# Output projection, FFN and q projection of a decode kernel with the weights as the moving operand, in four column tiles

## The chip, the cores and the metric

The kernel runs on one core of a Trainium2 chip. The metric is device time in microseconds (us) for one execution. Engines are named PE (matmul), DVE (vector), ACT (scalar), POOL (general) and SP (here it only issues transfers). A profile's span is some 2 us shorter than the time of the same run. A median is over all runs of a kernel, the slow ones too. A ratio is the mean time of one kernel's fast runs over that of the other's of the same rounds on the same chip, so it is not quite the ratio of the medians that are quoted beside it.

## The reference, cut to what matters

```python
# B = 4 tokens (batch), one position each, D = 448; 16 query heads, 8 KV heads, head size 256
# KV cache: 8192 positions, only the last W = 2048 are used; FFN width 1792; bf16
def A(x):                                # attention on the cache
    q = x @ wq                           # 448 -> 4096
    p = softmax(q @ k_window.T * 256**-0.5)
    return (p @ v_window) @ wo           # 4096 -> 448
def F(x):
    return (silu(x @ w_gate) * (x @ w_up)) @ w_down    # 448 -> 1792 -> 448
x = x + A(layernorm(x)); x = x + F(layernorm(x))
x = x + A(layernorm(x)); x = x + F(layernorm(x))       # same weights, same cache again
```

Two layers use the same cache window. A "pair" below is one token with one KV head in one layer: 1 MB of K and 1 MB of V, 64 pairs in all.

## The kernel before

The kernel is a graph of operations. A small planner, run when the program is built, gives each engine a fixed order. It is a greedy list scheduler: whenever an engine is free in the planner's own clock, it takes the ready operation with the lowest `rank`. The durations are constants in the source.

One pair. K is turned on DVE, the scores of 2048 positions are 32 matmuls, and the softmax goes from engine to engine: maximum on DVE, a broadcast matmul on PE, a second maximum on DVE, two exponentials on ACT. Two PSUM banks `Sb` are shared by all pairs in turn (NS = 2).

```python
MM = 0.0272                                          # planned us of one small matmul
...
g.op(PE, 32 * MM, pos - SLEAD, scores, ...)          # SLEAD = 1.5: before the previous pair's rank
g.op(DVE, 0.12, pos, lambda e: e.tensor_reduce(pmax[s_][:, :], Sb[s_][:, 0:32], AX.X, ALU.max, apply_transpose=True), ...)
g.op(PE, 0.1, pos, lambda e: e.matmul(Sb[s_][:, 128:256], lhsT=pmax[s_][:, 0:1].broadcast_to([128, 128]),
                                      rhs=identb[:, :], start=True, stop=True, ...), ...)        # the broadcast
g.op(DVE, 0.2, pos, lambda e: e.tensor_reduce(negm[s_][:, :], Sb[s_][:, 128:256]..., ALU.max, negate=True), ...)
for n in range(2):
    g.op(SCA, 0.17, pos, lambda e, n=n: e.activation(praw..., Sb..., ACT.Exp, bias=negm[s_][:, n:n + 1]), ...)
...
def pv(e, hv):                                       # already in four column tiles: V moves past 4 columns of p
    for a in range(2):
        for gg in range(4):
            last = e.matmul(Yb[p_][32 * gg:32 * gg + 4, 256:512], lhsT=pT..., rhs=half[vs[hv][0]]..., ...)
```

The small projections have the weights stationary, a 128x128 load for each matmul of 1 to 4 columns (the profile counts 5728 loads for 5728 matmuls in the whole kernel):

```python
def out_proj(pos, si, pairs):
    def emit(e):
        for cc in range(4):
            c0 = 128 * cc if cc < 3 else D - 128
            for k in range(4):
                last = e.matmul(Av[:, cc, sl], lhsT=wo_sb[:, 4 * kvh + k, c0:c0 + 128],
                                rhs=oT[si % 2][:, k % 2, k // 2, 0:n], start=False, stop=False, ...)
        return last
    g.op(PE, 16 * MM, pos, emit, ...)
...
def residual(t, rank):
    vec(rank, lambda e: e.tensor_tensor(xs[:, t, :], xs[:, t, :], Av[:, :, t], op=ALU.add), ...)
...
# when a token has finished a layer's 8 heads (rank CROSS = 20 positions ahead):
residual(t, pos); norm(t, pos, True)
if layer == 0:
    ffn(with_ + [t], pos)                            # gate, up 2 x 56 matmuls, down 56
    norm(t, pos, False)
    qproj([t], ((h0, 1), (h0 + 1, 1), (h0 + 2, HKV - h0 - 2), (0, h0)), pos)   # 128 matmuls, first head first
```

Transfers go into 15 buffers ("halves") of 512 KB. Five heads of each token stay in SBUF for the second layer; a held V half comes free when the second layer's pair has read it. The second layer of a token begins three steps into the next token.

Of the kernel before, what the change touches and what calls it, by code (L numbers as in the profile page):

```python
# [5 lines left out]
ACT = mybir.ActivationFunctionType  # L6
# [38 lines left out]
DSTART = 2.1  # L45
TAIL = {"pe": 0.2, "dve": 0.12, "act": 0.15, "pool": 0.1, "sp": 0.05}
# [232 lines left out]
def build(nc, A_x, A_k_cache, A_v_cache, A_wq, A_wo, B_x, B_w_gate, B_w_up, B_w_down, out):  # L279
# [3 lines left out]
    with ExitStack() as es:  # L283
# [12 lines left out]
        onesb = sb("onesb", [128, 128], BF16)  # L296
        rab = sb("rab", [128, 129], BF16)
        ra = [rab[:, 1:129], rab[:, 0:128]]
        esel = sb("esel", [128, 4, 4, 32], BF16)
        small = sb("small", [128, 9 + 2 * NS + 4 * NY], FP32)  # L300
# [5 lines left out]
        qmask = sb("qmask", [128, 4], BF16)  # L306
        qc = [sb(f"qc{t}", [128, HKV, 8, 2], BF16) for t in range(B)]
        qe = [sb(f"qe{i}", [128, 8, 4, 2], BF16) for i in range(NQ)]
        qS = sb("qS", [128, 8, 16], BF16)
        xio = KT[NKT - 1][:, 0:D]  # L310
        xio_k = tuple(f"kt{NKT - 1}_{hf}_{q}" for hf in range(2) for q in range(TRP))
        xs = sb("xs", [128, B, 4], FP32)
        st = sb("st", [128, B, 16], FP32)
# [4 lines left out]
        th = sb("th", [128, 2 * NFC], FP32)  # L318
        t1 = sb("t1", [128, 2 * NFC], FP32)
        hT = sb("hT", [128, 2 * NFC], BF16)  # L320
        pmax = [sb(f"pmax{s}", [128, 1], BF16) for s in range(NS)]
# [3 lines left out]
        osel = sb("osel", [128, 2], BF16)  # L325
        oT = [sb(f"oT{s}", [128, 2, 2, 2], BF16) for s in range(2)]
# [8 lines left out]
        Av = Ab[:, 0:16].rearrange("p (c t) -> p c t", t=B)  # L335

        R0 = -100.0
        MM = 0.0272
# [13 lines left out]
        def c_fill(e):  # L352
            e.memset(onesf[:, :], 1.0)
            e.memset(expo[:, 0:1], -0.5)
            e.memset(expo[:, 1:3], -1.0)
            e.memset(wrow[:, 0:3], 1.0 / D)
            e.memset(wrow[0:64, 3:4], 0.0)
            e.memset(wrow[64:128, 3:4], 1.0 / D)
            e.memset(qmask[:, :], 0.0)
            return e.memset(Ab[:, 0:16], 0.0)  # L360

        g.op(DVE, 0.5, R0, c_fill, w=("onesf", "expo", "wrow", "qmask") + tuple(f"acc{t}" for t in range(B)), bank=("A",))
# [6 lines left out]
        for a in range(4):  # L369
            g.op(DVE, 0.2, R0, lambda e, a=a: e.tensor_copy(  # L370
                esel[:, :, a, :], identb[:, :].rearrange("p (c s) -> p c s", c=4)), r=("identb",), w=(f"esel{a}",))
# [6 lines left out]
        for p_ in range(NY):  # L378
            g.op(DVE, 0.27, R0, lambda e, p_=p_: e.memset(Yb[p_][:, 256:512], 0.0), w=(f"y{p_}",), bank=(f"Y{p_}",))
        g.op(DVE, 0.2, R0, lambda e: e.memset(rab[:, :], 0.0), w=("ra",))  # L380
        g.op(DVE, 0.2, R0, lambda e: e.tensor_copy(
            rab[:, 1:129].rearrange("p (u v) -> p v u", v=2)[:, 0, :], identb[:, 64:128]), r=("identb",), w=("ra",))

# [10 lines left out]
        load(-80, 1 << 19, wq_sb[:, 3 * 4096:], A_wq[384:448, :].rearrange("r (h n) -> (r h) n", h=2), "wq3")  # L394
# [6 lines left out]
        def load_ffn(rank, rank_d):  # L401
            for nm, wsb, src in (("wg", wg_sb, B_w_gate), ("wu", wu_sb, B_w_up)):
                load(rank, 3 * 458752, wsb[:, 0:3 * FF].rearrange("p (c n) -> p c n", c=3),
                     src[0:384, :].rearrange("(c p) n -> p c n", p=128), nm + "a", 3584)
                load(rank, 229376, wsb[:, 3 * FF:], src[384:448, :].rearrange("r (h n) -> (r h) n", h=2), nm + "b")
            load(rank_d, 1605632, wd_sb[:, :, :], B_w_down.rearrange("(c p) n -> p c n", p=128), "wd", 896)
# [5 lines left out]
        def norm(t, rank, for_ffn):  # L412
# [3 lines left out]
            vec(rank, lambda e: e.scalar_tensor_tensor(out=s[:, 4:8], in0=xs[:, t, :], scalar=1.0, in1=wrow[:, :],  # L416
                                                       op0=ALU.mult, op1=ALU.mult, accum_out=s[:, 0:1]),
                (f"x{t}", "wrow"), (k + "w",), 0.18)
            vec(rank, lambda e: e.scalar_tensor_tensor(out=s[:, 4:8], in0=s[:, 4:8], scalar=1.0, in1=xs[:, t, :],
# [6 lines left out]
            vec(rank, lambda e: e.tensor_scalar(xn[:, :, t], xs[:, t, :], Z2[:, 0:1], None, op0=ALU.subtract),  # L426
# [3 lines left out]
            def spread(e):  # L430
                e.matmul(Z2[:, 16:17], lhsT=ra[0], rhs=xn[:, 3, t:t + 1], start=True, stop=False,
                         skip_group_check=True)
                return e.matmul(Z2[:, 17:18], lhsT=ra[1], rhs=xn[:, 3, t:t + 1], start=False, stop=True,
                                skip_group_check=True)
            g.op(PE, 0.06, rank, spread, r=(f"xn{t}", "ra"), w=("z2",), bank=("Z2",))
            vec(rank, lambda e: e.tensor_copy(xe[:, :, t], Z2[:, 16:18]), ("z2",), (f"xe{t}",), 0.1, ("Z2",))

# [7 lines left out]
            if for_ffn:  # L445
                gp(lambda e: e.tensor_single_scalar(s[:, 11:12], s[:, 8:9], 0.5, op=ALU.mult), (k + "r2",), (k + "s",))
                gp(lambda e: e.tensor_scalar(s[:, 14:15], s[:, 8:9], s[:, 11:12], None, op0=ALU.mult),
                   (k + "r2", k + "s"), (k + "t",))
# [5 lines left out]
        def qproj(ts, chunks, rank):  # L454

            n, sl = len(ts), span(ts)
            rn, rx = tuple(f"xn{t}" for t in ts), tuple(f"xe{t}" for t in ts)
            for i, (h0, nh) in enumerate(chunks):
                zb, z, bank = (Zb, "z", "Z") if i % 2 == 0 else (Z2, "z2", "Z2")

                def q_mm(e, zb, h0, nh, c0, c1):
                    last = None
                    for cc in range(c0, c1):
                        for hh in range(2 * nh):
                            for ee in range(2):
                                o = zb[:, (hh * 2 + ee) * n:(hh * 2 + ee + 1) * n]
                                if cc < 3:
                                    base, rhs = cc * 4096 + (2 * h0 + hh) * 256, xn[:, cc, sl]
                                else:
                                    h_ = 2 * h0 + hh  # L470
                                    base, rhs = 3 * 4096 + (h_ % 8) * 256, xe[:, h_ // 8, sl]
                                lhsT = wq_sb[:, base:base + 256].rearrange("p (m v) -> p v m", v=2)[:, ee, :]
                                last = e.matmul(o, lhsT=lhsT, rhs=rhs, start=(cc == 0 and hh == 0 and ee == 0),  # L473
                                                stop=(cc == 3), skip_group_check=True)
                    return last
                for c0, c1, rr, kw in ((0, 3, rn, dict(w=(z,))), (3, 4, rx, dict(acc=(z,)))):
                    g.op(PE, 4 * nh * (c1 - c0) * MM, rank,
                         lambda e, zb=zb, h0=h0, nh=nh, c0=c0, c1=c1: q_mm(e, zb, h0, nh, c0, c1),
                         r=rr + tuple(f"wq{c}" for c in range(c0, c1)), bank=(bank,), **kw)
                for j, t in enumerate(ts):  # L480
                    g.op(SCA, 0.18, rank, lambda e, zb=zb, j=j, t=t, i=i, nh=nh: e.activation(
                        qS[:, i * n + j, 0:4 * nh], zb[:, 0:4 * nh * n].rearrange("p (k t) -> p t k", t=n)[:, j, :],
                        ACT.Copy, scale=st[:, t, 8:9]), r=(z, f"st{t}r2"), w=(f"qS{i}_{j}",), bank=(bank,))
                for j, t in enumerate(ts):
                    def select(e, zb=zb, i=i, j=j, nh=nh):
                        last = None
                        src = qS[:, i * n + j, 0:4 * nh].rearrange("p (k h v) -> p k v h", h=2, v=2)
                        for c in range(4):
                            lhsT = esel[:, c, :, :].rearrange("p a s -> p (a s)")
                            o = zb[:, 128:128 + 16 * nh].rearrange("p (k c x) -> p k c x", c=4, x=4)[:, :, c, :]  # L490
                            last = e.matmul(o, lhsT=lhsT, rhs=src, start=(c == 0), stop=(c == 3),
                                            skip_group_check=True)
                        return last
                    g.op(PE, 0.12, rank, select, r=(f"qS{i}_{j}", "esel0", "esel1", "esel2", "esel3"), w=(z,),
                         bank=(bank,))
                    g.op(DVE, 0.06 + 0.016 * nh, rank, lambda e, zb=zb, h0=h0, nh=nh, t=t: e.tensor_copy(
                        qc[t][:, h0:h0 + nh, :, :].rearrange("p k c h -> p (k c h)"), zb[:, 128:128 + 16 * nh]),
                        r=(z,), w=tuple(f"qc{t}_{h}" for h in range(h0, h0 + nh)), bank=(bank,))

        def ffn(ts, rank):  # L500
            n, sl = len(ts), span(ts)
            gw = NFC * n

# [14 lines left out]
            for gi, (z, bank, w) in enumerate((("z", "Z", "wg"), ("z2", "Z2", "wu"))):  # L518
                g.op(PE, 42 * MM, rank, lambda e, gi=gi: gu(e, gi, 0, 3), r=rn + (w + "a",), w=(z,), bank=(bank,))
                g.op(PE, 14 * MM, rank, lambda e, gi=gi: gu(e, gi, 3, 4), r=rx + (w + "b",), acc=(z,), bank=(bank,))  # L520
# [3 lines left out]
            for j, t in enumerate(ts):  # L524
                g.op(SCA, 0.18, rank, lambda e, j=j, t=t: e.activation(
                    tok(th[:, 0:gw], j), tok(Zb[:, 0:gw], j), ACT.Tanh, scale=st[:, t, 11:12]),
                    r=("z", f"st{t}s"), w=(f"th{j}",), bank=("Z",))
# [295 lines left out]
```

## Time and profile before

| | before |
|---|---|
| time, median of 3 (lowest, highest) | 325.02 us (324.86, 327.12) |
| span of the profile | 322.9 us |
| matmuls, PE busy | 5728, 232.6 us |
| DVE busy, ACT busy | 192.6, 72.4 us |
| moved | 105.27 MB, mean 326 GB/s |

The page of the kernel before: the span, the busy time of the engines, PE and DMA in 40 slices of about 8 us, the rate of the transfers in the same slices, and the queue that the page calls "instruction" (packets, MB, share).

```profile
span 322.9 us, 12873 instructions
...
PE 232.6 (72%) x5728; PEld 169.7 (53%) x5728; DVE 192.6 (60%) x608; ACT 72.4 (22%) x289; POOL 84.9 (26%) x199
...
PE   3654454446588788578796895679787959889875
...
DMA  7999999999999999999889999999899999748000
GB/s 277 399 407 392 393 396 397 391 396 397 391 362 308 338 368 346 400 362 309 301 272 373 375 351 405 355 365 339 277 359 377 357 386 391 277 140 305 5 0 5
...
q8 instruction: 45, 0.74, 0.9%
```

Where transfers run freely they reach 393 to 407 GB/s. At that rate 105 MB need about 265 us (an estimate: 105.27 MB over 397 GB/s). The rest is a start, a tail with no transfers, and dips. The table of 8 us windows of the kernel before shows the dips after the FFN and q of tokens 0 and 1. Its columns are the window, its length, then busy us (instructions) of each engine, the recorded PE clock, the DMA share and GB/s:

```profile
...
core 0: us, PE busy (x) PEld busy (x) DVE busy (x) ACT busy (x) POOL busy (x), PEclk, DMA share, GB/s
...
96.00:104.00 8.00, 6.15 (x178) 4.94 (x178) 4.63 (x14) 1.61 (x7) 1.93 (x5) 1.00 0.88 296
144.00:152.00 8.00, 6.96 (x203) 5.68 (x200) 4.25 (x14) 1.10 (x4) 0.99 (x3) 1.00 0.89 309
152.00:160.00 8.00, 7.56 (x218) 5.95 (x219) 4.51 (x13) 2.34 (x9) 2.33 (x6) 1.00 0.89 313
160.00:168.00 8.00, 6.32 (x153) 4.18 (x149) 2.66 (x14) 2.11 (x9) 2.20 (x5) 1.00 0.81 277
```

The chain of waits of the kernel before has ten pieces over 0.6 us called "issue", 11.2 us in sum. They are of two kinds. In five of them (96.32, 160.25, 215.36, 226.38 and 278.44 us, 6.9 us in sum) PE really stands still for 0.83 to 1.68 us, and these are all such stops of PE over 0.6 us in the trace. The chain of waits of the kernel before has ten pieces over 0.6 us called "issue", 11.2 us in sum. The columns are start, us, what:

```profile
...
95.55 0.77 PE S L637 x29
96.32 1.22 issue
97.54 0.22 PE S L637 x3
```

Here PE stops within one run of 32 score matmuls, 0.2 us after a packet of 16 KB had come on the instruction queue (95.09 to 96.11 us). Such packets come about every 250 PE instructions (45 for 11456 matmuls and loads). That PE waits for instructions there is inferred from these times.

In the other five pieces (106.13, 117.40, 140.86, 194.13 and 248.15 us, 4.3 us in sum) no engine stops: DVE is at work on a transpose of K (L617) all the while, as a piece of the chain and the line of DVE's timeline for the same time show:

```profile
...
194.13 1.13 issue
...
```

```profile
...
194.09 1.25 DVE L617 STREAM_TRANSPOSE KT<-half 128x1024 uint32<-128x1024 uint32 x1 [0.80 <-DMA half<-in_A_k_cache_dram]
...
```

The groups of instructions that the argument needs, from the same kernel (busy us, mean ns of one | idle us before it and what ended it). The broadcast is L649; note 128*4 for the four column tiles of PV, 128*128 for the rest:

```profile
...
L677 PE MATMUL Y<-half,pT 128*4 128x256 bf16 x1024 | 70.0, 403 | 9.6 <-DMA half<-in_A_v_cache_dram 8.7 <-issue 0.8
L637 PE MATMUL S<-qe,KT 128*128 128x8 bf16 x2048 | 64.6, 168 | 22.4 <-DVE KT L617 18.5 <-issue 3.0 <-ACT praw L656 0.7
...
L649 PE MATMUL S<-identb,pmax 128*128 128x128 bf16 x64 | 16.6, 284 | 4.5 <-DVE pmax L646 3.6 <-DVE oT L702 0.7
...
L724 PE MATMUL A<-oT,wo_sb 128*128 128x1 bf16 x352 | 12.6, 166 | 2.3 <-DVE oT L702 2.3
```

The mean of one matmul (168 ns for L637) is longer than the distance to the next one's start, as one starts before the last has ended. What a stream costs is the distance between starts, which I take from the trace: 27 ns for the column matmuls of L637, L724, q and FFN, and about 170 or 213 ns from one group of four PV matmuls to the next.

### The profile page before, as it was taken

To read this page: it belongs to the slowest core of one execution; us is meant where nothing else is said; L and a number is where in the kernel's file an instruction comes from. 1 tells how busy PE (TensorE), PEld (TensorE's weight loads), DVE (VectorE), ACT (ScalarE), POOL (GpSimd) and SP (SyncE) were. 2 spreads that over 40 slices of the span, in tenths; PEclk is the share of its full clock that TensorE was granted. 3 is DMA by queue.
4 is the path that set the end of the run, shared out by engine and by line. 5 is a ranking of instruction groups with operands and counts; after the bars stand their busy time and mean duration, and the time that the engine had idled before them with its cause. 6 is when DMAs were issued, how large, how long until landed. Compare 5 with 4: busy or idle time off the path is not lost.

```text
span 322.9 us, 12873 instructions
## 1 busy us (share of the span) xinstructions
PE 232.6 (72%) x5728; PEld 169.7 (53%) x5728; DVE 192.6 (60%) x608; ACT 72.4 (22%) x289; POOL 84.9 (26%) x199
## 2 busy tenths in 40 slices
PE   3654454446588788578796895679787959889875
PEld 2542322234476465366664653567555636686554
DVE  5386555652145778765447787855377874656332
ACT  1112111111022333211231322113223322123310
POOL 3312111112023223240233331313233413134221
DMA  7999999999999999999889999999899999748000
GB/s 277 399 407 392 393 396 397 391 396 397 391 362 308 338 368 346 400 362 309 301 272 373 375 351 405 355 365 339 277 359 377 357 386 391 277 140 305 5 0 5
DMA packets 42327, 105.27 MB, mean 326 GB/s; under 512 B 3096, under 2 KB 7200, under 8 KB 41888
## 3 DMA queue, kind: packets, MB, share of 16 engines
q1 hardware_dynamic: 42272, 104.45, 88.0%
q8 instruction: 45, 0.74, 0.9%
q14 instruction: 10, 0.08, 0.1%
HBM read 104.44 MB, written 0.00 MB: 323 GB/s over the span
## 4 chain that ended last, share of the span: by engine, by line
DMA 38%; PE 34%; DVE 12%; SPq 7%; issue 5%; ACT 2%; POOL 0%; DVEq 0%
DMA half<-in_A_k_cache_dram 20%; DMA half<-in_A_v_cache_dram 12%; PE Y L677 11%; PE S L637 8%; DVE KT L617 6%; DMA wd_sb<-in_B_w_down_dram 5%; PE Z L473 4%; SPq L389 4%; PE A L724 3%; PE Z L514 3%; DVE oh L691 2%; PE Z L542 2%; SPq L609 2%; DVE small L652 2%; SPq L626 1%
## 5 line engine op out<-in xcount | busy, mean ns | idle before, releaser
L617 DVE STREAM_TRANSPOSE KT<-half 128x1024 uint32<-128x1024 uint32 x88 | 108.3, 1233 | 13.3 <-DMA half<-in_A_k_cache_dram 12.9
L637 PE MATMUL S<-qe,KT 128*128 128x8 bf16 x2048 | 64.6, 168 | 22.4 <-DVE KT L617 18.5
L677 PE MATMUL Y<-half,pT 128*4 128x256 bf16 x1024 | 70.0, 403 | 9.6 <-DMA half<-in_A_v_cache_dram 8.7
L637 PEld LDWEIGHTS S<-qe,KT 128*128 128x128 bf16 x2048 | 59.7, 104 | 30.7 <-DVE KT L617 20.8
L687 POOL TENSOR_TENSOR small<-small 128x2 f32<-128x2 f32 x64 | 44.3, 696 | 113.5 <-DVE small L669 103.3
L656 ACT ACTIVATE praw<-S,small 128x16 bf16<-128x16 f32 x128 | 28.7, 279 | 84.6 <-DVE small L652 83.9
L691 DVE SCALAR_TENSOR_TENSOR oh<-oh,small,Y 128x256 bf16<-128x256 bf16 x64 | 30.1, 472 | 23.9 <-ACT oh L689 23.4
L689 ACT ACTIVATE oh<-Y 128x256 bf16<-128x256 f32 x64 | 24.6, 384 | 74.2 <-PE Y L677 74.2
L641 POOL TENSOR_TENSOR qe<-qc,qmask 128x64 bf16<-128x64 bf16 x64 | 18.6, 294 | 71.3 <-PE S L637 52.3
L677 PEld LDWEIGHTS Y<-half,pT 128*4 128x4 bf16 x1024 | 20.0, 94 | 21.8 <-DMA half<-in_A_v_cache_dram 11.5
L646 DVE TRANSPOSE_TENSOR_REDUCE pmax<-S 128x1 bf16<-128x32 f32 x64 | 13.4, 211 | 27.1 <-PE S L637 25.3
L724 PE MATMUL A<-oT,wo_sb 128*128 128x1 bf16 (+1 forms) x688 | 24.8, 166 | 6.4 <-DVE oT L702 6.1
L724 PEld LDWEIGHTS A<-oT,wo_sb 128*128 128x128 bf16 x688 | 22.2, 105 | 10.5 <-DVE oT L702 8.5
L697 PE MATMUL Y<-osel,oh 128*128 128x2 bf16 x128 | 13.3, 173 | 17.4 <-DVE oh L691 17.2
L652 DVE TENSOR_REDUCE small<-S 128x2 f32<-128x128 f32 x64 | 17.4, 282 | 10.4 <-PE S L649 8.3
L666 ACT ACTIVATE pT<-Y 128x64 bf16<-128x64 f32 x64 | 14.1, 222 | 40.7 <-PE Y L663 40.4
L697 PEld LDWEIGHTS Y<-osel,oh 128*128 128x128 bf16 x128 | 8.8, 111 | 27.0 <-DVE oh L691 24.5
L649 PE MATMUL S<-identb,pmax 128*128 128x128 bf16 x64 | 16.6, 284 | 4.5 <-DVE pmax L646 3.6
L473 PE MATMUL Z<-xn,wq_sb 128*128 128x1 bf16 (+1 forms) x480 | 15.6, 165 | 2.6 <-DMA wq_sb<-in_A_wq_dram 1.9
L473 PEld LDWEIGHTS Z<-xn,wq_sb 128*128 128x128 bf16 x480 | 14.3, 104 | 3.4 <-DMA wq_sb<-in_A_wq_dram 2.0
L669 DVE TENSOR_REDUCE small<-Y 128x2 f32<-128x32 f32 x64 | 11.0, 177 | 7.1 <-ACT pT L666 6.8
L440 POOL TENSOR_SCALAR st<-st 128x1 f32<-128x1 f32 x16 | 4.3, 267 | 41.2 <-DVE st L428 40.7
(76 smaller groups left out, 212.0 us busy)
## 6 DMA issues: line engine op xcount, KB each, us to landing
half<-in_A_k_cache_dram SPq DMA_DIRECT2D x88, 512.0 KB, 7.0
half<-in_A_v_cache_dram SPq DMA_DIRECT2D x88, 512.0 KB, 6.7
wo_sb<-in_A_wo_dram SPq DMA_DIRECT2D x8, 448.0 KB, 12.3
wq_sb<-in_A_wq_dram SPq DMA_DIRECT2D x3, 1024.0 KB, 6.9
wd_sb<-in_B_w_down_dram SPq DMA_DIRECT2D x1, 1568.0 KB, 16.3
wg_sb<-in_B_w_gate_dram SPq DMA_DIRECT2D x1, 1344.0 KB, 14.2
wu_sb<-in_B_w_up_dram SPq DMA_DIRECT2D x1, 1344.0 KB, 14.7
wq_sb<-in_A_wq_dram SPq DMA_DIRECT2D x1, 512.0 KB, 10.4
```

The source lines that it names most:

```text
L473: last = e.matmul(o, lhsT=lhsT, rhs=rhs, start=(cc == 0 and hh == 0 and ee == 0), stop=(cc == 3), skip_group_check=True)
L617: return e.transpose(dst[:, 2 * hf + q * n:2 * hf + q * n + n], src[:, q * n:q * n + n])
L637: last = e.matmul(Sb[s_][:, 8 * gg:8 * gg + 8], lhsT=kt[:, gg, ce // 2, ce % 2, :], rhs=qe[q_][:, ce, :, :], start=(gg == 0 and ce == 0), ...
L641: g.op(POOL, 0.25, pos - SLEAD - 1, lambda e: e.tensor_tensor(qe[q_][:, :, :, :], qc[t][:, kvh, :, :].unsqueeze(2).broadcast_to([128, 8, 4 ...
L652: g.op(DVE, 0.2, pos, lambda e: e.tensor_reduce(negm[s_][:, :], Sb[s_][:, 128:256].rearrange("p (k n) -> p n k", n=2), AX.X, ALU.max, nega ...
L656: g.op(SCA, 0.17, pos, lambda e, n=n: e.activation(praw[s_][:, :].rearrange("p (k n) -> p n k", n=2)[:, n, :], Sb[s_][:, 0:32].rearrange(" ...
L677: last = e.matmul(Yb[p_][32 * gg:32 * gg + 4, 256:512], lhsT=pT[p_][:, 4 * gg + 2 * hv + a, :, :].rearrange("p y n -> p (y n)"), rhs=half[ ...
L687: g.op(POOL, 0.25, pos, lambda e: e.tensor_tensor(ri[p_][:, :], rs[p_][:, :], expo[:, 1:3], op=ALU.pow), r=(f"rs{p_}", "expo"), w=(f"ri{p_ ...
L689: g.op(SCA, 0.28, pos, lambda e: e.activation(oh[p_][:, :], Yb[p_][:, 256:512], ACT.Copy), r=(f"y{p_}",), w=(f"oh{p_}",), bank=(f"Y{p_}",))
L691: g.op(DVE, 0.4, pos, lambda e: e.scalar_tensor_tensor(out=oh[p_][:, :], in0=oh[p_][:, :], scalar=lomask[:, 0:1], in1=Yb[p_][:, 256:512], ...
L697: last = e.matmul(Yb[p_][:, 2 * dh:2 * dh + 2], lhsT=oh[p_][:, :].rearrange("p (m e) -> p e m", e=2)[:, dh, :], rhs=osel[:, :], start=Fals ...
L724: last = e.matmul(Av[:, cc, sl], lhsT=wo_sb[:, 4 * kvh + k, c0:c0 + 128], rhs=oT[si % 2][:, k % 2, k // 2, 0:n], start=False, stop=False, ...
```

## The change

The intent is fewer and longer matmuls. With four tokens at most, an activation has 4 columns. If it is the stationary operand, the weights move past it 448 or 512 columns at a time, and four of these matmuls write to the four 32-row strips of one PSUM bank. Output projection falls from 16 matmuls to 4, gate and up from 112 to 34, q from 128 to 32. Results then lie as rows, in four strips that have to be summed and turned back into columns by further matmuls. The residual sum of the output projection and of the down projection stays in PSUM as rows. The last step of each token's layer, token 3's FFN and the last FFN stay in columns. The planner's cost of a small matmul goes from 0.0272 to 0.04 us.

```diff
+ROWF = (0, 1, 2)
+MMV = 0.04
...
-        MM = 0.0272
+        MM = MMV
...
         def out_proj(...):
+            def row(e):
+                for k in range(4):
+                    last = e.matmul(Ab[32 * k:32 * k + B, 0:D], lhsT=oT[si % 2][:, k % 2, k // 2, :],
+                                    rhs=wo_sb[:, 4 * kvh + k, :], start=False, stop=False, skip_group_check=True)
+            if column:
+                g.op(PE, 16 * MM, pos, col, ...)
+            else:
+                g.op(PE, 0.4, pos, row, ...)
...
+        def rows(t, rank):                      # strips -> columns, as a bf16 high and low part
+            g.op(SCA, 0.55, rank, lambda e: e.activation(wideb[:, 0:D], Ab[:, 0:D], ACT.Copy), ...)
+            vec(rank, lambda e: e.tensor_tensor(wideb[:, 512:512 + D], Ab[:, 0:D], wideb[:, 0:D], op=ALU.subtract), ...)
+            def turn(e):
+                for i in range(2):
+                    for cc in range(4):
+                        c0 = 512 * i + (128 * cc if cc < 3 else D - 128)
+                        last = e.matmul(Zb[:, cc:cc + 1], lhsT=wideb[:, c0:c0 + 128], rhs=rsel[:, t:t + 1], ...)
+            g.op(PE, 0.25, rank, turn, ...)
+            vec(rank, lambda e: e.tensor_tensor(xr[:, t, :], xs[:, t, :], Zb[:, 0:4], op=ALU.add), ...)
...
-        def qproj(ts, chunks, rank):
+        def qproj(ts, rank):                    # two banks of 4 strips x 512, copied by ACT, turned, selected
+                        for j in range(4):
+                            last = e.matmul(zb[32 * j:32 * j + B, 0:512], lhsT=xn[:, cc, :], rhs=wq_sb[:, c:c + 512], ...)
...
+        def ffn_row(ts, rank):                  # gate, up; tanh and two DVE passes over 512; turn; down into the rows
+            g.op(SCA, 0.65, rank, lambda e: e.activation(wide[:, :], Zb[:, :], ACT.Tanh, scale=rvec[:, 2:3]), ...)
+            vec(... wide = (wide + 1) * Zb ...);  vec(... wideb = wide * rvec * Z2 ...)
+            g.op(PE, 0.12, rank, turn, ...);      vec(... hT = Zb[:, 0:64] ...)
+            g.op(PE, 1.5, rank, down, ...)
...
             for t, layer in full:
+                rows(t, pos - CROSS)
+            out_proj(pos, si, pairs, bool(full))
...
-                    ffn(with_ + [t], pos)
+                    if t in ROWF:
+                        ffn_row(with_ + [t], pos)
+                        for u in with_ + [t]:
+                            rows(u, pos)
+                            residual(u, pos)
+                    else:
+                        ffn(with_ + [t], pos)
                     norm(...)
-                    qproj([t], ((h0, 1), (h0 + 1, 1), (h0 + 2, HKV - h0 - 2), (0, h0)), pos)
+                    qproj([t], pos)
```

Cut: the layout of the last 64 rows of the weights, constants, small buffers merged to make room, and a clearing of the oT buffers on POOL.

## The prediction

> **What bounds the kernel now.** Mostly the transfers. The page moves 105.27 MB; 8 us stretches full of transfers run at 393 to 407 GB/s, so the data alone needs about 265 of the 322.9 us. By the table of 8 us windows the other 58 are: about 3 at the start, 25 after 296 us (DMA share 0.27, then 0.01), and 30 in dips after each token's FFN and q projection (88-128, 144-176, 208-240, 248-264, 272-296 us; share 0.61 to 0.95). In the dips PE shows 6.4 to 7.5 us busy of 8, and the DMA queue's own waits are for PE and DVE work that frees K/V halves. Only there and in the tail can this change pay.
>
> **PE cost now (raw start times, groups by line).** A 128x128 load with a 1- or 2-column matmul issues every 27 to 29 ns: output projection 16 in 0.43 us, q 128 in 3.6, FFN 168 in 4.7. Such bursts also use up instructions: an instruction-queue packet of 16 KB comes every ~250 PE instructions (45 packets), and PE shows "issue" gaps of 0.7 to 1.7 us just after such packets in dense bursts (96.3, 106, 117, 141, 160, 194, 215, 226, 278 us), 10.5 us in sum. [...]
>
> **Cost of the new form.** The PV product already uses four column tiles: its groups of four 256-column matmuls start 213 ns apart[...]. [...] Scaled, a group of four takes 0.37 us at 448 columns, 0.43 at 512. Output projection 0.37 against 0.43 (35 of 43 steps: -2 us); q 3.4 against 3.6; FFN about 5 against 4.7. Streaming saves nearly nothing. What falls is matmuls, 5728 to about 4580, instruction packets, 45 to about 36, and the bursts: I expect two thirds of the 10.5 us of gaps to go.
>
> **Added.** Twelve turns of rows (ACT 448 columns ~0.57 us, DVE ~0.65, eight small matmuls, an add: ~2 us of latency; ~8 us of DVE in all); in the three row FFNs a tanh and two DVE passes over 512 columns (~0.7 each) and a turn; in q two copies of ~0.6 and a turn. Residual to first score takes some 5 us longer; three steps (16 us of transfers) lie between, so for tokens 1 and 2 it is partly hidden; token 0's tail behind the down weights (landed 85.4 us) grows 2 us. The last FFN stays in columns; the tail moves under 1.5 us.
>
> **Sum.** -2 (output projection) and -7 (gaps) of PE time, half to three quarters of which reaches the span, +2 for DVE and longer chains, tail -0.5. Some -6 us, with a wide margin since the whole static order changes (the planner's matmul cost goes from 0.0272 to 0.04): **319 us, 311 to 328**; faster 0.45, same 0.46, slower 0.09.
>
> **Right if** matmuls ~4580, instruction packets ~36; PE "issue" gaps over 0.6 us fall from nine to about three; groups of four 512-column matmuls start ~430 ns apart; DMA rate in 144-168 and 208-240 rises by 20 to 40 GB/s; DVE busy +8 us; tail unchanged.
>
> **Wrong if** [...] the gaps aren't fetches; the rows' chain delays second-layer scores so that held halves free later (slower); the new order moves the transfers.

The sizes of the row matmuls are scaled from the measured 213 ns. The durations given for ACT and DVE on 448 and 512 columns were estimates. The trace after has a mean of 541 ns (ACT) and 613 ns (DVE) for 448 columns, 688 ns for the tanh, 662 and 719 ns for the two DVE passes and 687 ns for a copy of q, all of 512. The twelve turns, from ACT's start to the end of the add, take 2.20 to 10.77 us.

## More of the kernel before

On the chip each engine is given its list, with a wait wherever data may be missing. PE keeps to it: in the trace of this kernel the 531 runs of matmuls of one source line start in the order of the program. A wrong duration therefore adds no instruction; it moves instructions in the lists.

```python
# the planner's core (cut)
while n < len(self.ops):
    ...                                              # engine e that can start first, at time t
    o = min((o for o in avail[e] if ready_at[o] <= t + 1e-9), key=lambda o: (o.rank, o.i))
    o.start = t
    free[e] = t + o.dur                              # o.dur: a constant from the source
    o.end = t + o.dur
    ...
    order[e].append(o)                               # the engine's list on the chip
```

## The result, and the profile after

| | before | after |
|---|---|---|
| time, median of 5 (lowest, highest) | 325.02 us (324.15, 327.12) | 351.48 us (348.07, 352.28) |
| ratio, 95% interval | | 1.0789 (1.073 to 1.0847) |
| span of the profile | 322.9 us | 346.0 us |
| matmuls | 5728 | 4584 |
| PE, DVE, ACT busy | 232.6, 192.6, 72.4 us | 238.7, 206.2, 80.3 us |
| "issue" over 0.6 us in the chain of waits | 10, 11.2 us | 5, 5.0 us |
| of these with PE standing still | 5, 6.9 us | none |

The change makes the kernel 8% slower. The same lines of the page as before, and the recorded clock of PE in tenths:

```profile
span 346.0 us, 10675 instructions
...
PE 238.7 (69%) x4584; PEld 138.1 (40%) x4584; DVE 206.2 (60%) x637; ACT 80.3 (23%) x286; POOL 88.1 (25%) x227
...
PE   2654544555497887676877776787796959769855
...
PEclk9999999999995555558665555555655555565555
DMA  7999999999978999899959899999489999626000
GB/s 287 352 401 395 395 393 392 397 367 329 393 283 275 376 367 329 323 346 335 334 202 334 302 396 357 339 360 351 175 289 387 364 327 351 233 69 240 2 1 4
...
q8 instruction: 36, 0.59, 0.7%
```

The counts are as intended, 4584 matmuls and 36 instruction packets, but the transfers have deeper holes. Selected 8 us windows of the changed kernel:

```profile
...
core 0: us, PE busy (x) PEld busy (x) DVE busy (x) ACT busy (x) POOL busy (x), PEclk, DMA share, GB/s
96.00:104.00 8.00, 7.42 (x142) 3.66 (x140) 1.90 (x9) 2.57 (x6) 2.01 (x9) 1.00 0.78 274
...
176.00:184.00 8.00, 6.78 (x162) 4.89 (x159) 7.15 (x23) 2.02 (x8) 3.58 (x11) 0.50 0.52 177
...
248.00:256.00 8.00, 6.72 (x144) 4.47 (x141) 7.13 (x18) 2.03 (x8) 3.22 (x9) 0.50 0.50 168
304.00:312.00 8.00, 5.68 (x159) 4.59 (x159) 7.08 (x22) 1.11 (x5) 4.01 (x13) 0.60 0.32 101
```

The DMA queue's own waits say what it waits for: without the wait of the last store, in sum 149.8 us for DVE and 69.8 for PE, against 121.6 and 79.1 before. DVE must turn K before a K half comes free. In the 8 us ahead of the hole at 176 us it is busy for only 2.7 us, and waits 3.5 us for the matmuls that turn q's rows; in the hole itself it is busy for 7.15 of 8 us.

The time is lost all along. I cut both traces at the addition that ends the first layer of each token (its start on DVE):

| from - to | before | after | difference |
|---|---|---|---|
| start - token 0 | 76.2 us | 77.1 us | 0.9 |
| token 0 - token 1 | 60.2 | 66.9 | 6.7 |
| token 1 - token 2 | 67.3 | 71.9 | 4.6 |
| token 2 - token 3 | 66.3 | 71.1 | 4.8 |
| token 3 - end | 52.9 | 59.0 | 6.1 |

Groups of the changed kernel. 128*4 now stands on the output projection (L838) and q (L488) too; L756 is the broadcast, L644 and L646 make the two parts of the rows:

```profile
...
L838 PE MATMUL A<-wo_sb,oT 128*4 128x448 bf16 x140 | 18.3, 524 | 4.5 <-DVE oT L809 3.4 <-DVE xr L662 1.1
...
L756 PE MATMUL S<-identb,tiny 128*128 128x128 bf16 x64 | 16.0, 288 | 4.7 <-DVE tiny L753 4.6
L488 PE MATMUL Z<-wq_sb,xn 128*4 128x512 bf16 x120 | 14.6, 620 | 0.8 <-DMA wq_sb<-in_A_wq_dram 0.5 <-DVE st L440 0.3
...
L646 DVE TENSOR_TENSOR wide<-A,wide 128x448 bf16<-128x448 f32 x12 | 7.4, 613 | 5.4 <-ACT wide L644 5.4
...
L644 ACT ACTIVATE wide<-A 128x448 bf16<-128x448 f32 x12 | 6.5, 541 | 15.0 <-PE A L578 10.1 <-PE A L838 3.1 <-DVE xr L662 1.8
```

### The clock line, and why it is not the cause

The page says that PE had its full clock before, and half of it from the 13th slice on after. That reading is wrong, and it invites a false story. The trace of the kernel before holds no clock record at all, which is shown as 1.00. The distances give the clock away: a group of four PV matmuls, 256 columns each, starts about 170 or 213 ns after the last, and the longer distance is 1.2 columns a ns. In the changed kernel the first record is at 100.87 us. The record says "full" for six stretches of 3.4 us, each of which begins during a dense burst of rows or within 1.4 us of its end, and the eight distances between PV groups that lie in them are 108 to 110 ns, 2.3 to 2.4 columns a ns; everywhere else they are 166 to 171 or 212 to 215 ns, two or three strays aside, with the record at 0.5 or with no record yet. So by the distances both kernels run PE at half the clock nearly all the time. The run b_burst, below, tests it with a dense burst at the start of the kernel before, since in the changed kernel the record begins with a stretch at the end of one.

This also corrects a reading from the prediction: it took 213 ns as four tiles at only twice the rate of one. They run at once: the four of a group start within 16 ns of each other, and 256 columns in 213 ns is 1.2 columns a ns for each of them, the same as for matmuls that run singly (107 ns from start to start for 128 columns in b_burst). The sizes drawn from it held all the same, since the other groups run at the same 1.2 columns a ns: groups of four 512-column matmuls most often start 427 ns apart.

### The profile page after: what moved, and what is told of

Its sections match the earlier page's. It is cut to its first block, busy times and chain, and to the rows that moved or that the text cites. A ratio compares the mean times of both kernels' runs of the same rounds, so it can differ in the third digit from the quotient of the medians.

```text
span 346.0 us, 10675 instructions
## 1 busy us (share of the span) xinstructions
PE 238.7 (69%) x4584; PEld 138.1 (40%) x4584; DVE 206.2 (60%) x637; ACT 80.3 (23%) x286; POOL 88.1 (25%) x227
## 4 chain that ended last, share of the span: by engine, by line
DMA 40%; PE 34%; DVE 16%; ACT 4%; issue 4%; SPq 3%; POOL 0%; DVEq 0%
DMA half<-in_A_k_cache_dram 21%; DMA half<-in_A_v_cache_dram 19%; PE Y L784 10%; PE S L744 8%; DVE KT L724 7%; PE Z L488 4%; DVE oh L798 2%; PE Z L604 2%; DVE small L759 2%; PE A L838 1%; SPq L716 1%; ACT oh L796 1%; PE Y L804 1%; PE Z L434 1%; PE Y L767 1%
## 5 line engine op out<-in xcount | busy, mean ns | idle before, releaser
L724 DVE STREAM_TRANSPOSE KT<-half 128x1024 uint32<-128x1024 uint32 x88 | 108.2, 1230 | 17.8 <-DMA half<-in_A_k_cache_dram 17.6
L763 ACT ACTIVATE praw<-S,small 128x16 bf16<-128x16 f32 x128 | 27.6, 278 | 60.8 <-DVE small L759 60.2
L753 DVE TRANSPOSE_TENSOR_REDUCE tiny<-S 128x1 bf16<-128x32 f32 x64 | 13.7, 214 | 30.3 <-PE S L744 29.9
L748 POOL TENSOR_TENSOR qe<-qc,tiny 128x64 bf16<-128x64 bf16 x64 | 18.4, 292 | 47.0 <-PE S L744 23.9
L804 PE MATMUL Y<-tiny,oh 128*128 128x2 bf16 x128 | 13.4, 174 | 21.5 <-DVE oh L798 21.3
L838 PE MATMUL A<-wo_sb,oT 128*4 128x448 bf16 x140 | 18.3, 524 | 4.5 <-DVE oT L809 3.4
L804 PEld LDWEIGHTS Y<-tiny,oh 128*128 128x128 bf16 x128 | 8.9, 113 | 31.0 <-DVE oh L798 28.7
L756 PE MATMUL S<-identb,tiny 128*128 128x128 bf16 x64 | 16.0, 288 | 4.7 <-DVE tiny L753 4.6
L767 PE MATMUL Y<-praw,permb 128*128 128x32 bf16 x64 | 12.7, 205 | 7.8 <-ACT praw L763 7.6
L767 PEld LDWEIGHTS Y<-praw,permb 128*128 128x128 bf16 x64 | 6.5, 103 | 27.2 <-ACT praw L763 16.0
L488 PE MATMUL Z<-wq_sb,xn 128*4 128x512 bf16 x120 | 14.6, 620 | 0.8 <-DMA wq_sb<-in_A_wq_dram 0.5
L809 DVE TENSOR_TENSOR oT<-Y,small 128x4 bf16<-128x4 f32 x64 | 10.2, 160 | 8.2 <-PE Y L804 7.9
```

Source lines behind the costliest of these rows:

```text
L488: last = e.matmul(zb[32 * j:32 * j + B, 0:512], lhsT=lhsT, rhs=wq_sb[:, c:c + 512], start=(cc == 0), stop=(cc == 3), skip_group_check=True)
L724: return e.transpose(dst[:, 2 * hf + q * n:2 * hf + q * n + n], src[:, q * n:q * n + n])
L763: g.op(SCA, 0.17, pos, lambda e, n=n: e.activation(praw[s_][:, :].rearrange("p (k n) -> p n k", n=2)[:, n, :], Sb[s_][:, 0:32].rearrange(" ...
L767: g.op(PE, 0.03, pos, lambda e: e.matmul(Yb[p_][:, 64:96], lhsT=permb[:, :], rhs=praw[s_][:, :], start=True, stop=False, skip_group_check= ...
L804: last = e.matmul(Yb[p_][:, 2 * dh:2 * dh + 2], lhsT=oh[p_][:, :].rearrange("p (m e) -> p e m", e=2)[:, dh, :], rhs=osel[:, :], start=Fals ...
L838: last = e.matmul(Ab[32 * k:32 * k + B, 0:D], lhsT=oT[si % 2][:, k % 2, k // 2, :], rhs=wo_sb[:, 4 * kvh + k, :], start=False, stop=False, ...
```

## The experiments

All 18 kernels gave a correct result. Two theories about the result were on the table first. The chain theory: the rows add links between engines to the chain from a token's residual to its next q, so held halves come free later. The planner theory: the cost of 0.04 alone moved the fixed order of all engines to a worse one. The clock theory was a third.

| run | what | median us | before, same rounds | ratio (95% interval) |
|---|---|---|---|---|
| a_ffncol | change, FFN in columns, 0.04 | 342.13 | 326.00 | 1.0536 (1.0454 to 1.0619) |
| q_rows_only | only q in rows, 0.04 | 338.42 | 326.00 | 1.0378 (1.0325 to 1.0432) |
| out_rows_only | only output projection in rows, 0.04 | 349.12 | 326.00 | 1.0668 (1.0597 to 1.0739) |
| b_plan40 | before, planned at 0.04 | 336.00 | 326.00 | 1.0294 (1.0236 to 1.0352) |
| a_plan27 | change, planned at 0.0272 | 330.88 | 327.22 | 1.0112 (1.0048 to 1.0176) |
| b_delay6 | before, +6 us latency on 3 chains | 334.68 | 327.22 | 1.0199 (1.0114 to 1.0284) |
| b_delay12 | before, +12 us latency on 3 chains | 344.41 | 327.22 | 1.0557 (1.0467 to 1.0647) |
| b_burst | before, a burst of matmuls at the start | 325.41 | 327.22 | 0.9943 (0.9841 to 1.0046) |
| a_scores27 | change, only the scores planned at 0.0272 | 332.59 | 325.08 | 1.0188 (1.0098 to 1.0279) |
| b_scores40 | before, only the scores planned at 0.04 | 334.23 | 325.08 | 1.0265 (1.0216 to 1.0315) |
| a_ffncol_27 | change, FFN in columns, 0.0272 | 332.56 | 325.08 | 1.0228 (1.0167 to 1.0289) |
| out_rows_only_27 | only output projection in rows, 0.0272 | 335.02 | 325.08 | 1.0293 (1.021 to 1.0376) |
| a40_boost | change, 0.04, broadcast ranked first | 334.44 | 325.88 | 1.0272 (1.0197 to 1.0347) |
| b_boost | before, broadcast ranked first | 323.83 | 325.88 | 0.9945 (0.9868 to 1.0021) |
| b_plan22 | before, planned at 0.022 | 328.48 | 325.88 | 1.0087 (1.0011 to 1.0162) |
| q_rows_only_27 | only q in rows, 0.0272 | 328.55 | 325.88 | 0.9980 (0.9874 to 1.0086) |
| a27_boost | change, 0.0272, broadcast ranked first | 329.30 | 325.81 | 1.0172 (1.0118 to 1.0226) |
| q_rows_boost | q in rows, 0.0272, broadcast ranked first | 325.53 | 325.81 | 1.0050 (0.9994 to 1.0107) |

### Undoing parts of the change: a_ffncol, q_rows_only, out_rows_only

```diff
 # a_ffncol
-ROWF = (0, 1, 2)
+ROWF = ()
 # q_rows_only: as a_ffncol, and
-                rows(t, pos - CROSS)
-            out_proj(pos, si, pairs, bool(full))
+                vec(pos - CROSS, lambda e, t=t: e.tensor_copy(xr[:, t, :], xs[:, t, :]), ...)
+            out_proj(pos, si, pairs, True)
 # out_rows_only: as a_ffncol, with the column q of before (its selection as 16 matmuls of 32 columns, for want of room)
```

> The changed kernel with its three row FFNs back in columns (output projection and q stay in rows). Chain theory (the row FFN adds links between engines; from the residual to the first q of the second layer tokens 1 and 2 took 30.9 and 30.4 us against 18.7 and 18.9 before): the chain shortens by 7 to 9 us for each of three tokens, and the span falls to 330 to 340 us. Planner theory (the order planned with a matmul cost of 0.04 is what hurts): stays within 345 to 352. Clock theory (the record of a half clock is the cause): the record stays below 0.8 and the time above 343.

> The changed kernel with FFN and every output projection in columns: only q is in rows, with the planner's cost at 0.04. Chain theory: the residual-to-q chain is 4 to 6 us longer than before for each token, the span 326 to 334 us. Planner theory: still 340 or more. If 323 to 326, q in rows costs nothing and the loss lies in the other two parts.

> The changed kernel with FFN and q in columns: only the output projection is in rows, turned once for each token and layer ahead of the last step's columns. Chain theory: the turn lies off the chain, 322 to 329 us. Planner theory: 340 or more. A theory that the rows' DVE and ACT work itself costs: 330 to 336.

The three gave 342.13, 338.42 and 349.12 us. No part brings the loss back to 325, and the parts don't add up: output projection in rows alone is slower than output projection and q in rows together. No theory fits all three: 342.13 lies between the ranges of all of them (the profiled span, 338.7, is just within the chain theory's), 338.42 misses the chain theory's (up to 334) and the planner theory's (from 340), and only 349.12 is as one of them said, the planner theory. Something common to all three is at work.

### The planner's cost: b_plan40, a_plan27, a_scores27, b_scores40, b_plan22

```diff
 # b_plan40 (before)                 # b_plan22: 0.022
-        MM = 0.0272
+        MM = 0.04
 # a_plan27 (after)
-MMV = 0.04
+MMV = 0.0272
 # a_scores27 (after)                # b_scores40 (before): 32 * 0.04
-            g.op(PE, 32 * MM, pos - SLEAD, scores, ...)
+            g.op(PE, 32 * 0.0272, pos - SLEAD, scores, ...)
```

> The kernel before with one edit: the planner's cost of a matmul 0.0272 becomes 0.04. No instruction is added, only the static order moves. Planner theory: 338 or more. Chain theory: within 2%, 320 to 331 us.

> The changed kernel with the planner's matmul cost back at 0.0272. Planner theory: 335 or less. Chain theory: stays within 343 to 358.

> The changed kernel in which only the planner's duration of the 32 score matmuls goes back from 1.28 to 0.87 us (the trace has 0.83 to 0.95); everything else planned at 0.04. Theory that the over-long scores spoil the order: 327 to 335 us, like the run with the whole constant put back (330.9). Theory that the planned cost of the column FFN or of the last output projection matters: 340 or more.

> The kernel before in which only the score matmuls are planned as 1.28 us in place of 0.87. Over-long scores theory: most of the 10 us that the whole constant cost it, 331 to 340 us. Otherwise (the FFN, q and output projection planned too long are what cost): 323 to 328.

> The kernel before planned with matmuls too short (0.022 in place of 0.0272). Theory that any order away from the tuned constant costs the same: 331 or more, like 0.04. Theory that only durations planned too long push the softmax chain back: 322 to 329.

These runs add and remove no instruction. The changed kernel planned at 0.0272 takes 330.88 us in place of 351.48: of the 26.5 us by which it was slower, 20.6 were the constant (by the ratios, 6.8 of 7.9%). The kernel before loses 10 us with the new constant. It fell short of the 338 that the planner theory had asked of b_plan40, so the same constant costs the changed kernel twice what it costs the old one.

Nearly all of it is in the scores. With only the scores planned at 0.87 us the changed kernel takes 332.59; with only the scores planned at 1.28 the old one takes 334.23. In all traces a run of 32 score matmuls takes 0.78 to 0.87 us from its first start to its last when it isn't held up, 25 to 28 ns for each; so 0.0272 is right for them and 0.04 wrong. A constant that is too small (0.022, by a factor of 1.24; 0.04 is too large by 1.47) costs 0.9%, so not every other order costs as much; a constant too small by 1.47 was not tried.

The page of a_plan27 shows the dips filled to about what they were before: the slice with 175 GB/s is gone, and the lowest in mid-span is 282.

```profile
span 328.5 us, 10661 instructions
...
GB/s 280 355 403 393 394 395 396 392 397 318 360 364 283 282 390 352 402 347 348 368 348 350 390 393 354 294 375 362 324 283 385 391 385 346 269 66 259 2 2 3
```

### How a duration in the planner costs time on the chip: a40_boost and b_boost

From the start times of the trace I took, for pairs 9 to 64, the wait from the end of the maximum on DVE to the broadcast matmul on PE, how many of the 56 waits are over 2 us, and the time from the first score matmul to the end of the exponentials, in which one of two S banks is taken:

| kernel | mean wait us | over 2 us | scores to exponentials us | ratio |
|---|---|---|---|---|
| before | 1.23 | 14 | 4.54 | |
| b_plan40 | 2.32 | 23 | 5.51 | 1.0294 |
| b_scores40 | 1.96 | 26 | 5.11 | 1.0265 |
| after | 1.44 | 17 | 4.67 | 1.0789 |
| a_plan27 | 1.00 | 6 | 4.11 | 1.0112 |
| a_scores27 | 1.12 | 8 | 4.29 | 1.0188 |
| a40_boost | 0.39 | 1 | 3.80 | 1.0272 |
| b_boost | 0.74 | 3 | 4.10 | 0.9945 |

The timeline of the changed kernel shows one such wait. The columns are start, us, engine, line, operation, out<-in, count:

```profile
...
322.46 0.99 PE L744 MATMUL S<-qe,KT 128*128 128x8 bf16 x32
...
323.38 1.02 PE L784 MATMUL Y<-half,pT 128*4 128x256 bf16 x16
323.49 0.22 DVE L753 TRANSPOSE_TENSOR_REDUCE tiny<-S 128x1 bf16<-128x32 f32 x1 [0.39 <-PE S L744]
...
324.41 0.99 PE L744 MATMUL S<-qe,KT 128*128 128x8 bf16 x32
...
325.44 0.22 DVE L753 TRANSPOSE_TENSOR_REDUCE tiny<-S 128x1 bf16<-128x32 f32 x1
...
325.55 1.03 PE L784 MATMUL Y<-half,pT 128*4 128x256 bf16 x16
...
326.36 0.59 PE L838 MATMUL A<-wo_sb,oT 128*4 128x448 bf16 x4
...
326.88 0.40 PE L756 MATMUL S<-identb,tiny 128*128 128x128 bf16 x2
...
327.44 0.48 DVE L759 TENSOR_REDUCE small<-S 128x2 f32<-128x128 f32 x2
...
327.76 0.77 ACT L763 ACTIVATE praw<-S,small 128x16 bf16<-128x16 f32 x4 [0.75 <-DVE small L759]
```

The maximum of the first pair (L753) is ready at 323.71. Its broadcast (L756) runs at 326.88, because the list of PE has PV, the next pair's 32 scores, another PV and an output projection ahead of it; then it runs together with that of the next pair. The matmuls of this trace start in the order of the list, by source line, but for eight FFN matmuls that start among those of PV in two places (153.4 to 154.2 and 224.3 to 225.1 us). In the planner's clock, scores of 1.28 us leave the broadcast waiting for a busy PE, so it can put more between. It also ranks the next pair's scores (pos + 1 - 1.5) ahead of this pair's broadcast (pos).

The experiment is one edit of one rank:

```diff
-            g.op(PE, 0.1, pos, lambda e: e.matmul(            # the broadcast
+            g.op(PE, 0.1, pos - SLEAD - 1, lambda e: e.matmul(
                 Sb[s_][:, 128:256], lhsT=pmax[s_][:, 0:1].broadcast_to([128, 128]), rhs=identb[:, :], ...
```

> The full change with its planner cost of 0.04 kept; one edit: the broadcast matmul of each pair's running maximum gets a rank ahead of the next pair's scores. No instruction is added or removed. In the traces so far the wait from the maximum on DVE to this matmul was 1.44 us here, 2.32 and 2.19 in two other kernels planned at 0.04, 1.0 to 1.23 in those planned at 0.0272. Broadcast theory: that wait falls to about 1 us and the span to 330 to 338. If it stays at 345 or more, the broadcast is a symptom and the cause lies elsewhere in the order.

> The kernel before with the same one-rank edit, planner cost 0.0272. Broadcast theory: the wait there is already 1.23 us, so a small gain, 318 to 325 us. If it is slower by over 2%, a rank away from the tuned order costs by itself.

The changed kernel, with its 0.04 kept, falls from 351.48 to 334.44 us. The wait falls to 0.39 us. The timeline of a40_boost shows the broadcast following its maximum although the scores and PV of other pairs are about:

```profile
...
260.52 1.02 PE L744 MATMUL S<-qe,KT 128*128 128x8 bf16 x32
...
261.01 0.21 DVE L753 TRANSPOSE_TENSOR_REDUCE tiny<-S 128x1 bf16<-128x32 f32 x1
...
261.45 0.27 PE L756 MATMUL S<-identb,tiny 128*128 128x128 bf16 x1
261.57 0.22 DVE L753 TRANSPOSE_TENSOR_REDUCE tiny<-S 128x1 bf16<-128x32 f32 x1 [0.35 <-PE Y L804]
...
261.65 1.02 PE L784 MATMUL Y<-half,pT 128*4 128x256 bf16 x16
...
262.61 0.29 PE L756 MATMUL S<-identb,tiny 128*128 128x128 bf16 x1
```

and the rate of its transfers, in the page's 40 slices, has no slice under 266 GB/s in mid-span:

```profile
span 331.6 us, 10661 instructions
...
GB/s 274 364 403 393 394 396 394 393 399 309 370 370 266 318 393 373 390 294 342 362 380 327 355 384 388 326 324 359 288 308 374 395 376 367 209 74 248 2 2 3
```

So the rank of one matmul in each pair, with all that it moves in the lists, is worth about 17 of the 26.5 us, and the DMA queue's waits for DVE fall from 149.8 to 132.1 us. Two limits. The edit of the rank also moves what follows in the list, so it isn't proof that the wait by itself has this price. The planner, run again without the chip for pairs 9 to 64, gives its lists: between the scores of a pair and its broadcast it puts 4.7 other operations of PE on average in the changed kernel, 4.4 in a_plan27 and 3.0 in a40_boost, but 6.9 in b_plan40 against 4.6 before. The constant thus pushes the broadcast back in both kernels, only a little in the changed one, which lost more by it. And the table's wait doesn't rank different kernels: b_plan40 waits longer than the changed kernel and is faster, and b_boost brings the wait down from 1.23 to 0.74 with no gain that is clear of noise. That the wait counts only where pairs, and not the transfers, set the pace is a guess.

### Latency alone: b_delay6, b_delay12

```diff
                     ffn(with_ + [t], pos)
+                    for _ in range(20 if t < B - 1 else 0):        # b_delay12: 40
+                        g.op(POOL, 0.25, pos, lambda e, t=t: e.tensor_single_scalar(xs[:, t, :], xs[:, t, :], 1.0, op=ALU.mult), ...)
                     norm(t, pos, False)
```

> The kernel before with 20 multiplications by one on POOL (4 columns each, about 0.28 us) in the chain between FFN and the second norm of tokens 0, 1 and 2: latency alone, about 6 us, no PE or DVE work. Chain theory: each token's second layer starts some 6 us later and held halves free later; the span grows by 8 to 18 us, to 333 to 343. A theory that the engines' added work is what costs (DVE +14, ACT +8, PE +6 us busy): under 4 us, 323 to 329.

> The same with 40 multiplications, about 12 us for each of three tokens, which is what the changed kernel's chain grew by for tokens 1 and 2. Chain theory: 345 to 362 us, that is most of the changed kernel's loss from latency alone. Added-work theory: under 332.

Latency between the FFN and the second norm does cost: 7.5 and 17.2 us by the medians; the second run, 344.41 us, ends just under the range of the chain theory. From a token's residual to the first copy of its new q, b_delay12 has 28.9, 31.4 and 29.3 us for tokens 0 to 2, against 14.8, 18.7 and 18.9 before. The chain is thus near its slack, and 37.2 us of added latency in sum cost 17.2.

That chain grew in the changed kernel too: 25.6, 30.9 and 30.4 us, and 17.6 against 13.0 for token 3, whose FFN stayed in columns. But it is not where most of the loss came from. In a40_boost it is still 26.0, 25.0, 29.4 and 17.6 us, only token 1's is clearly shorter, and 17 us of the span are back. In a_plan27 it is 26.5, 24.9, 28.4 and 17.2. By the price of latency in b_delay12 the 27.4 us that tokens 0 to 2 have more than before would come to about 13 us, an estimate; a_plan27 lost 3.7 by the medians. If that estimate holds, something in the rows gives some of it back. The stops of PE called "issue" are a candidate: one of 0.8 us in a_plan27 against five with 6.9 us before. It wasn't tested alone, and b_boost speaks against a high price: its stops are ten with 12.9 us, and it is no slower than the kernel before.

### The clock: b_burst

```diff
+        def burst(e):
+            for i in range(56):
+                last = e.matmul(Sb[0][:, 0:128], lhsT=identb[:, :], rhs=identb[:, :], start=True, stop=True, ...)
+        g.op(PE, 3.0, R0 - 1, burst, r=("identb",), w=("s0", "m0"), bank=("S0",))
```

> The kernel before with 56 matmuls of 128 columns ahead of the first norm, where PE waits for the q weights. If a missing clock record means full clock, nothing changes in the record (1.00) and PV groups stay 213 ns apart. If the kernel before runs at the half clock all along and is only never recorded, [...] the record then says about 0.5 for the rest of the span, and PV groups are 213 ns apart as before; the time stays within 1% of before either way. Clock theory of the loss: a kernel recorded at about 0.5 must be some 8% slower, near 350.

The burst, 107 ns from start to start (128 columns, 1.2 a ns), brought a stretch recorded at the full clock, from 7.7 to 11.1 us of the span. From there the page says 0.5 to the end:

```profile
span 322.2 us, 12984 instructions
...
PEclk9655555555555555555555555555555555555555
```

The run took 324.02 us, and PV groups are about 170 or 213 ns apart as before. A kernel recorded at 0.52 of the clock is as fast as the one recorded at 1.00, and by these distances they had the same clock. The clock theory falls.

### What the rows cost with the order repaired: a_ffncol_27, out_rows_only_27, q_rows_only_27

The edits are those above with `MMV = 0.0272`.

> The changed kernel planned at 0.0272 and with the FFNs in columns: only output projection and q are in rows. Chain theory of what is left (3.6 us over before): the row FFN is the longest addition to the chain, so this falls below the 330.9 us of the full change, to 325 to 329. If 330 or more, the row FFN is not what is left.

> Only the output projection in rows, planned at 0.0272. Same theory: the turn lies off the chain, 324 to 329 us. If it is 333 or more, the output projection in rows costs by itself, whatever the plan (planned at 0.04 it took 349.1, 13 us over the kernel before planned at 0.04).

> Only q in rows, planned at 0.0272. q gives its first head 4 us later after its start than the chunked form did (6.5 against 2.6 us at token 1), so 325 to 331; near 325 would mean that q in rows costs nothing and what is left of the loss comes from the output projection in rows (335.0 alone).

q in rows is neutral (0.998). The output projection in rows alone costs 2.9%, with q in rows 2.3%, and with the row FFN as well 1.1%. The expectation that the row FFN is the part that still costs was wrong: putting it back into columns didn't help. I had held the output projection for harmless, since its turn is off the chain; it is the part with a price of its own. Why stays open. Its group of four takes 373 ns by the distances of the down projection's like groups, against 16 x 27 = 432 ns, both estimates, so PE has little to gain from it. The selection in 16 matmuls, which out_rows_only does four times for a token, is hardly the reason: a_ffncol_27 does it once for a token and costs 2.3%, and q_rows_only_27 does the same and is neutral. POOL's new waits before it clears the oT buffers are not either: they sum to 16.1 us in out_rows_only_27 and to 20.5 us in q_rows_only_27, which is neutral.

### A version that beats both? a27_boost, q_rows_boost

> The full change planned at 0.0272 and with the broadcast ranked ahead of the next pair's scores. The two repairs act on the same wait, so they should not add up: 326 to 332 us. If 322 or less, the rows gain once the order is right; if 334 or more, the rows have a cost of their own that the order does not touch.

> Only q in rows, planned at 0.0272, broadcast ranked ahead: candidate to beat both kernels. 320 to 327 us; the kernel before with the same rank edit took 323.8 (0.9945 of before).

Neither does. The two repairs don't add up (329.30 us with both, 330.88 and 334.44 with one), as they act on the same wait. q in rows with both is level with before. No version tried here beats the kernel before beyond noise; the best is b_boost at 0.9945 with an interval that includes 1.

## Why the prediction was wrong, point by point

- "Some -6 us ... 319 us, 311 to 328": measured 351.48 us, +26.5. The step that failed first is the last clause of the sum, "with a wide margin since the whole static order changes (the planner's matmul cost goes from 0.0272 to 0.04)". It was noted and given no sign and no size. a_plan27 puts it at 20.6 of the 26.5 us, a_scores27 shows that it is the scores, and a40_boost wins 17 back by the rank of the broadcast alone; how much of that is the broadcast's own wait stays open. The trace before had already shown that 32 scores take 0.83 to 0.85 us from first start to last, so a planned 1.28 could have been called wrong before the run.
- "Wrong if ... the new order moves the transfers": this case came true.
- "-7 (gaps) of PE time, half to three quarters of which reaches the span": the term was too large from the start. Of the nine gaps that the prediction lists, four (106, 117, 141 and 194 us) are DVE at work on a K transpose; PE stood still in five, 6.9 us in sum. These did go: none is left in the changed kernel, one of 0.8 us in a_plan27. No net gain reached the span: with the order repaired the change is 1.1% slower, not 1.9% faster. What the stops cost by themselves was not measured.
- "Residual to first score takes some 5 us longer": mis-sized. Measured to the first copy of q it took 10.9, 12.2 and 11.5 us longer for tokens 0 to 2 (11.7, 6.1 and 9.5 with the order repaired). I had added durations and left out the queueing at each of the added links, where the engine is busy with a pair (the turns of the rows alone take 2.20 to 10.77 us).
- "DVE busy +8 us": +13.6. The figure held only the twelve row passes (0.613 us each, 7.4 in sum) and left out the two passes over 512 columns of each row FFN, which the same paragraph lists (six of 0.65 to 0.75 us, 4.1 in sum).
- "the tail moves under 1.5 us": from token 3 to the end it is 6.1 us longer, 3.4 in a_plan27 (56.3 against 52.9).
- Right: matmuls about 4580 (4584), packets about 36 (36), groups of four 512-column matmuls about 430 ns apart (427), and that streaming saves nearly nothing. The reason given for the last was wrong: the four tiles run at once (starts within 16 ns), at 1.2 columns a ns each where the clock is recorded at 0.5. The rate in 144-168 and 208-240 us rose by 34 and 23 GB/s on average, as forecast, but that is luck: the work had moved in time, and holes opened beside them (176-184 us from 393 to 177 GB/s, 248-256 from 350 to 168).
- Partly right: "only in the dips and the tail can this change pay". They are also where it lost.

## What to carry to other kernels

A planner constant is part of a change even if no instruction comes of it: check each planned duration against the trace before, and run the old kernel with the new constant and the new kernel with the old one before explaining anything by the instructions. In fixed lists, try a rank ahead of the next item's long bursts for the short links of a chain (one matmul between two reductions); here it won 17 us in an order spoilt by a wrong constant and nothing clear of noise in the tuned one. Before a piece of the chain called "issue" is taken for a stop, look at what its engine does in that time. Read the clock from the distance between matmuls of known width, not from a clock column that may have no record under it (here up to 213 ns for 256 columns where the page shows 1.00 with no record, 108 to 110 ns where the full clock is recorded).
